# Forgetting attention with a gated FFN: the causal mask as rows of the score contraction

## The chip, the cores and the metric

The kernel runs on one core of a Trainium2 chip. A core has a matrix engine (TensorE, PE in the profile), a vector engine (VectorE, DVE), an activation engine (ScalarE, ACT), a general engine (GpSimd, POOL) and a queue engine (SyncE, SP), each of which works through its own instructions in order; here nearly all DMAs are issued by SP. The metric is the device time of one execution in microseconds; less is better. It is given as the median of the runs.

## What is computed

Eight batches of eight heads, 576 positions, head dimension 64. Attention with a decay that is a cumulative sum of log f, a causal mask, and then a feed-forward part over the heads side by side (512 channels, 1024 hidden), gated by the sigmoid of a three-tap convolution along the sequence:

```
scores = scale * q @ k.T
decay  = cum[:, :, :, None] - cum[:, :, None, :]      # cum = cumsum(log(clip(f, 1e-4, 1)))
scores = where(key later than query, -1e9, scores + decay)
x      = softmax(scores) @ v                          # heads side by side: 512 channels
h      = relu(x @ w_in)
out    = (h * sigmoid(conv3(h, conv_w))) @ w_out
```

## The kernel before

**Work.** Attention goes by half batches, hb 0 to 15, of four heads each; the FFN goes by batches b 0 to 7 once both half batches are done. Scores are made with keys on the partitions. The five diagonal blocks of a head (four of 128x128, one of 64x64) and the off-diagonal ones are separate groups: `sd` makes the diagonal blocks of two heads, `so` the off-diagonal ones of one head, `st` the 64x64 tails of four heads. `ed`, `eo` and `et` are their exponentials on ACT (L353, L370, L332). `pv` multiplies with v (L389, L394; a column of ones gives the softmax sum), `n` and `m` normalise on VectorE (L403, L405), `t` turns the result on PE (L414) and `tx` copies it (L417). Per batch and 128 hidden channels ff, `f` is the first FFN matmul (L429), `r` the relu (L440, ACT), `c` and `d` the two convolution steps (L446, L448, VectorE), `a` the tanh or sigmoid (L451, ACT), `g` the gate (L458, or L456 for the last ones, VectorE). `o` is the second matmul (L474), `e` copies it out (L479, L484), `s` stores it.

**How q and k come in.** A tile `qk` (a ring of four) holds q and k of a half batch with the contraction on 128 partitions. The fp32 input is read as pairs of 16-bit words and transposed by the DMA (L180): the odd partitions then hold the upper words, which are q or k in bf16, and the even ones hold the lower words, which are no use. Those 64 even rows are taken for other things. Three of them carry the decay: q rows hold cum or one, k rows the counterpart, so that the score matmul adds the decay by itself. The other even rows must be zero. In hb 2 to 7 VectorE multiplies by a mask of odd partitions and sets the ones (`cl`, L186), and `rw` writes the decay rows by DMA from an image in DRAM (L202, L203). In hb 8 to 15 a DMA writes zeros over 60 even rows (L194) and another the four rows of the image (L196); SP does it all in `fi`. Half batches 0 and 1 are loaded plainly, turned by PE (`tp`, L166) and copied out by ACT or VectorE with the same clamp (`cl`, L172, L174). hb 0 gets its decay by two more matmuls a score block (L315, L317).

**How the mask is made.** In hb 0 to 7 (`MASK_PE`) a matmul of an identity with a tile of 0 and -1e30 (L320) opens each group of diagonal blocks: one of 512 columns for four blocks, one of 256 for the tails. In hb 8 to 15 the exponentials of the diagonal blocks are written unmasked in fp32 (`pd`, `p3`), and POOL selects them into the fp16 tile with zeros above the diagonal (`md`, `mt`, L356, L335).

**What sets the order.** A long hand-written table, ORDER, lists all tasks; each engine gets its instructions in that order, and buffers are handed out by it. `PSUM` is four tiles of 1024 columns, taken by every group of scores, every `pv`, `t`, `f` and `o`. `x@DVE` in the table names the engine where there is a choice.

## Time and profile before

| | us |
|---|---|
| median of 3 runs | 247.38 |
| lowest, highest | 247.0, 248.49 |
| span of the profiled execution | 244.1 |
| between span and median | 3.3 |

The span runs from the first to the last instruction of the profiled execution, whose own time outside the profiler isn't listed; the rest up to the median is taken as a constant around the span. The profile gives for each group of instructions the line, the engine, the operation and what it writes and reads, the count, the busy time, the mean duration, and the idle time of the engine ahead of it with what ended that idle time. Consecutive instructions of an engine overlap in their records, so the duration of one in a dense stream is read from start to start.

### The profile page before, as it was taken

Reading aid. Unit: us, or ns where it says so; the run is one execution under the profiler, and the core shown is the slowest. Engines: PE = TensorE matmul, PEld = TensorE weight load, DVE = VectorE, ACT = ScalarE, POOL = GpSimd, SP = SyncE. Lnnn points to the kernel's source line nnn. Section 1 sums busy time; section 2 is a strip of 40 time slices with the busy share of each in tenths; the row PEclk is TensorE's granted clock in tenths of the full one; section 3 lists DMA queues with packets and bytes.
Section 4 is the critical chain, followed back from the end, with each engine's and each line's share of the span. In section 5 each row is a group of like instructions: output and inputs, shape, how many; then the busy total and the mean of one; then the engine's idle time right before and its main releaser. Section 6 shows DMA issues by size and latency. Waiting matters only on the chain.

```text
span 244.1 us, 6385 instructions
## 1 busy us (share of the span) xinstructions
PE 226.9 (93%) x2627; PEld 145.0 (59%) x2627; DVE 205.1 (84%) x323; ACT 206.9 (85%) x278; POOL 52.9 (22%) x77
## 2 busy tenths in 40 slices
PE   0899899779999999999999999999999999999991
PEld 0787585547556676575557755675666566444440
DVE  5735359999998999999999889996998889999931
ACT  2868677999998999999999999999988995798442
POOL 8020520205220020030402570245311311000000
PEclk9999999999999999999999999999999999999999
DMA  6999999999999999999999999969999950641326
GB/s 192 328 159 243 304 204 192 202 253 279 204 188 205 228 158 240 229 314 186 198 256 246 187 209 257 273 134 222 194 260 188 236 140 3 168 157 62 142 86 216
DMA packets 120176, 49.68 MB, mean 204 GB/s; under 512 B 109759, under 2 KB 110271, under 8 KB 120147
## 3 DMA queue, kind: packets, MB, share of 16 engines
q1 hardware_dynamic: 119981, 48.97, 92.4%
q8 instruction: 20, 0.33, 0.6%
q10 hardware_dynamic: 166, 0.31, 0.4%
q14 instruction: 9, 0.07, 0.1%
HBM read 21.11 MB, written 10.17 MB: 128 GB/s over the span
## 4 chain that ended last, share of the span: by engine, by line
PE 78%; DVE 7%; DMA 6%; ACT 4%; issue 1%; ACTq 1%; SPq 1%; DVEq 0%
PE ps L474 24%; PE ps L429 20%; PE ps L312 15%; PE ps L389 7%; DMA qk<-in_q_dram 3%; PE ps L320 3%; PE ps L394 3%; PE ps L166 2%; PE ps L414 2%; DVE u L446 2%; ACT pp L370 2%; DMA pd<-in_moe_conv_w_dram 2%; DVE u L448 2%; DVE qk L186 1%; DMA qk<-image 1%
## 5 line engine op out<-in xcount | busy, mean ns | idle before, releaser
L429 PE MATMUL ps<-xt,w_in_f 128*128 128x512 f16 (+1 forms) x512 | 69.9, 286 | 0.0
L370 ACT ACTIVATE pp<-ps 128x1024 f16<-128x1024 f32 x64 | 64.7, 1032 | 4.2 <-PE ps L312 2.7
L474 PE MATMUL ps<-w_out_f,hg 128*128 128x512 f16 x288 | 66.8, 379 | 0.0
L312 PE MATMUL ps<-qk 128*128 128x128 bf16 (+2 forms) x576 | 63.4, 240 | 1.6 <-ACT pp L353 0.8
L446 DVE SCALAR_TENSOR_TENSOR u<-ht,cwt 128x576 f32<-128x576 f16 x64 | 52.7, 837 | 3.6 <-ACT ht L440 3.4
L451 ACT ACTIVATE hg<-u,cw 128x576 f16<-128x576 f32 x64 | 48.7, 782 | 5.9 <-DVE u L448 5.8
L448 DVE SCALAR_TENSOR_TENSOR u<-ht,cwt,u 128x576 f32<-128x576 f16 x64 | 53.2, 846 | 0.5
L429 PEld LDWEIGHTS <-w_in_f 128*128 128x128 f16 x512 | 34.3, 98 | 28.5
L312 PEld LDWEIGHTS <-qk 128*128 128x128 bf16 x576 | 39.2, 98 | 19.8 <-issue 3.3
L440 ACT ACTIVATE ht<-ps 128x576 f16<-128x576 f32 x64 | 41.0, 663 | 6.0 <-DVE hg L458 2.7
L474 PEld LDWEIGHTS <-hg 128*128 128x128 f16 x288 | 26.9, 98 | 28.8
L458 DVE SCALAR_TENSOR_TENSOR hg<-hg,ht 128x576 f16<-128x576 f16 x51 | 38.7, 771 | 0.6 <-ACT hg L451 0.5
L356 POOL TENSOR_SCALAR_AFFINE_SELECT pp<-pd 128x1024 f16<-128x1024 f32 x16 | 19.7, 1244 | 53.6 <-ACT pd L353 53.6
L389 PE MATMUL ps<-va,pp 128*128 128x65 f16 x640 | 24.8, 193 | 1.1 <-DVE va L217 1.0
L389 PEld LDWEIGHTS <-pp 128*128 128x128 f16 x640 | 22.6, 97 | 3.7 <-DVE va L217 1.3
L405 DVE TENSOR_TENSOR xm<-ps,rc 128x896 f16<-128x896 f32 (+1 forms) x32 | 23.9, 751 | 0.5
L353 ACT ACTIVATE pp<-ps 128x1024 f16<-128x1024 f32 x16 | 16.6, 1039 | 4.7 <-PE ps L312 3.9
L353 ACT ACTIVATE pd<-ps 128x1024 f32<-128x1024 f32 x16 | 16.2, 1023 | 1.2 <-PE ps L312 1.0
L217 POOL CAST va<-vf 128x1024 f16<-128x1024 f32 x8 | 10.0, 1252 | 32.1 <-DMA vf<-in_v_dram 27.8
L320 PE MATMUL ps<-mask,ident 128*128 128x512 bf16 (+1 forms) x40 | 14.3, 359 | 1.5 <-ACT pp L370 0.8
L403 DVE RECIPROCAL rc<-ps 128x14 f32<-128x14 f32 (+1 forms) x32 | 6.7, 208 | 8.6 <-PE ps L394 5.5
L479 ACT COPY ob<-ps 128x1024 f32<-128x1024 f32 (+1 forms) x14 | 12.9, 919 | 0.3 <-issue 0.2
(83 smaller groups left out, 176.4 us busy)
## 6 DMA issues: line engine op xcount, KB each, us to landing
vf<-in_v_dram SPq DMA_DIRECT2D x32, 256.0 KB, 7.7
out_dram<-ob SPq DMA_DIRECT2D x14, 512.0 KB, 3.7
qk<-blank SPq DMA_DIRECT2D x8, 540.0 KB, 6.2
ob<-in_moe_w_in_dram SPq DMA_DIRECT2D x4, 512.0 KB, 6.3
ob<-in_moe_w_out_dram SPq DMA_DIRECT2D x4, 512.0 KB
out_dram<-ob SPq DMA_DIRECT2D x6, 256.0 KB, 7.2
vf<-in_v_dram SPq DMA_DIRECT2D x8, 128.0 KB, 5.9
hg<-in_q_dram SPq DMA_DIRECT2D x2, 288.0 KB
```

The costliest lines, as they stand in the source:

```text
L312: nc.tensor.matmul(o, tk[:, h * S + k0:h * S + k0 + 128], tq[:, h * S + q0:h * S + q0 + n], start=first, stop=last and not by_matmul(hb, h))
L353: nc.scalar.activation(o, ps_of(f"sd{i}").rearrange("p (s c) -> p s c", s=2), AF.Exp, scale=SCALE)
L370: nc.scalar.activation(pair(i)[:, s, 512:1536], ps_of(f"so{i}.{s}"), AF.Exp, scale=SCALE)
L389: nc.tensor.matmul(ps[:, c:c + D + 1], block(hb, h, m, n), va[:, h, m, 0:D + 1], start=(m == 0), stop=(m == n))
L405: nc.vector.tensor_tensor(xm[:, CUT * D * u:CUT * D * u + nj * k * D].rearrange("p (j x d) -> p j x d", x=k, d=D), got[:, :, :, 0:D], r.un ...
L429: nc.tensor.matmul(ps[:, t0:t1], w_in_f16[:, cc, 128 * ff:128 * (ff + 1)], xt[:, cc // 2, x:x + t1 - t0], start=(cc == 0), stop=(cc == NCC ...
L440: nc.scalar.activation(ht_of(b, ff)[:, 2:2 + S], ps_of(f"f{b}.{ff}")[:, 0:S], AF.Relu, scale=1.0 if (b, ff) in LATE else 0.5)
L446: nc.vector.scalar_tensor_tensor(u, ht[:, 1:1 + S], cwt[:, ff, 0:1], ht[:, 2:2 + S], op0=ALU.mult, op1=ALU.add)
L448: nc.vector.scalar_tensor_tensor(u, ht[:, 3:3 + S], cwt[:, ff, 1:2], u, op0=ALU.mult, op1=ALU.add)
L451: nc.scalar.activation(hg_of(b, ff), u_t[slot[f"c{b}.{ff}", "u"]], AF.Sigmoid if (b, ff) in LATE else AF.Tanh, scale=cw[:, ff, 1:2])
L458: nc.vector.scalar_tensor_tensor(hv, hv, 1.0, ht_of(b, ff)[:, 2:2 + S], op0=ALU.add, op1=ALU.mult)
L474: nc.tensor.matmul(ps[:, 512 * (c % 2):512 * (c % 2 + 1)], w, w_out_f16[:, ff, :], start=(ff == 0), stop=(ff == NFF - 1))
```

## The change

The mask becomes part of the score contraction in hb 1 to 15. Sixty rows beside q and k now hold steps of powers of two (`steps_q`, `steps_k`, made at the start by VectorE from counters that POOL lays out), such that the products sum to a large negative number where the key of a diagonal block is later than the query, and to next to nothing elsewhere. Only hb 0 keeps the mask matmul.

- hb 1: rows 64 to 123 of its `qk` tile hold the steps (`edge_rows` spreads them over the heads), 124 to 127 the decay rows.
- hb 2 to 7 (`BLEND`): VectorE clears the even rows (`blanked`, `cl`) and adds the tile `edge` in a second pass (`blend`, `cb`).
- hb 8 to 15: the DMA that wrote zeros writes the steps from a DRAM copy, `shape`.
- The decay rows are four in every half batch, with q and k sides in one DMA (`rows_of`).
- hb 0 and 1 are turned as bf16 alone, 64 rows, and copied without the clamp.
- The selects on POOL with their fp32 tiles go; the exponentials write fp16 directly. `st` and `et` use 64 partitions.
- f is loaded by SP (`lf`), behind one load of k, and the conv weights go first on ACT's queue. `sel_k` and `sel_q` are made by POOL, in place of VectorE.
- ORDER is another one; engines of copies and casts in it change too.

```diff
 ORDER = """
-dca cw ld0 ld1 ld0.0.0 tp0.0.0 dcl ld0.1.0 ld0.0.1 tp0.0.1 tp0.1.0 v0.0 ld0.1.1
+ld0 ks ld1 ld0.0.1 lf ld0.0.0 ld1.0.0 ld1.0.1 cw pz ld0.1.1 ld0.1.0 gu dca mk dcl gw
...
+    BLEND = (2, 3, 4, 5, 6, 7,)
-    MASK_PE = (0, 1, 2, 3, 4, 5, 6, 7,)
...
-            nc.tensor.transpose(o[:, 128 * j:128 * (j + 1)], i[:, 128 * j:128 * (j + 1)], ident_b)
+            nc.tensor.transpose(o[0:64, 128 * j:128 * (j + 1)], i[:, 128 * j + 1:128 * (j + 1):2], ident_b)
...
-    def clamp(hb, h0, nh, side):
-        t = (stq_t, stk_t)[side][hb % RING].bitcast(U16)[:, h0 * S:(h0 + nh) * S]
-        nc.vector.tensor_scalar(t, t, lim[:, 2 * side:2 * side + 1], lim[:, 2 * side + 1:2 * side + 2],
-                                op0=ALU.mult, op1=ALU.add)
+    def blanked(hb, side):
+        t = (stq_t, stk_t)[side][hb % RING].bitcast(U16)[:, 0:HS]
+        nc.vector.tensor_scalar(t, t, lit[:, 2:3], None, op0=ALU.mult)
+
+    def blend(hb, side):
+        t = (stq_t, stk_t)[side][hb % RING][:, 0:HS].rearrange("p (h s) -> p h s", h=HH)
+        nc.vector.tensor_tensor(t, t, edge[:, side].unsqueeze(1).broadcast_to((128, HH, S)), op=ALU.add)
+
+    def edge_rows(side, e):
+        copy = {"ACT": nc.scalar.copy, "POOL": nc.gpsimd.tensor_copy, "DVE": nc.vector.tensor_copy}[e]
+        o = qk_t[1][64:128, HS * side + S:HS * (side + 1)].rearrange("p (h s) -> p h s", s=S)
+        copy(o, qk_t[1][64:128, HS * side:HS * side + S].unsqueeze(1).broadcast_to((64, HH - 1, S)))
...
     def fill(hb):
-        nc.sync.dma_start(even_rows(hb, 4, 60, 0, 2 * HS).rearrange("p (h s) -> p h s", s=2 * S),
-                          blank.unsqueeze(1).broadcast_to((60, HH, 2 * S)))
+        nc.sync.dma_start(rows(qk_t[hb % RING], 0, 2, 60, 0, 2 * HS).rearrange("p (a h s) -> p a h s", a=2, s=2 * S),
+                          shape.rearrange("p a h s -> p a (h s)").unsqueeze(2).broadcast_to((60, 2, 2, 2 * S)))
+        rows_of(hb)
...
-    nc.scalar.dma_start(fsb[0:BH], f.rearrange("b h s -> (b h) s"))
-    nc.scalar.dma_start(fsb[BH:128], f.rearrange("b h s -> (b h) s"))
     nc.scalar.preload_act_table(AF.Ln)
     nc.scalar.dma_start(cwrow, moe_conv_w)
+    def load_f():
+        for h in range(2):
+            nc.sync.dma_start(fsb[BH * h:BH * (h + 1)], f.rearrange("b h s -> (b h) s"))
...
+    def steps_q():
+        nc.vector.tensor_scalar(near, count, GROUP + (FAR + 0.003) / STEP, None, op0=ALU.min)
+        nc.vector.scalar_tensor_tensor(bits, near, float(-128 * STEP), base, op0=ALU.mult, op1=ALU.add)
+        nc.vector.scalar_tensor_tensor(there, near, 0.0, bits, op0=ALU.is_ge, op1=ALU.mult)
+        nc.vector.scalar_tensor_tensor(dense[0], near, GROUP - 0.5, there, op0=ALU.is_le, op1=ALU.mult)
+
+    def steps_k():
+        nc.vector.tensor_scalar(bits, bits, -1.0, float(128 * (FIRST - STEP + 2 * 127) + 32768), op0=ALU.mult, op1=ALU.add)
+        nc.vector.scalar_tensor_tensor(dense[1], near, 1.0, bits, op0=ALU.is_ge, op1=ALU.mult)
+
+    def spread():
+        t = qk_t[1][64:128, 0:2 * HS].rearrange("p (a c) -> p a c", a=2)[:, :, 0:S]
+        nc.sync.dma_start(bass.AP(tensor=edge.tensor, offset=int(edge.offset), ap=[[2 * 2 * S, 64], [S, 2], [1, S]]), t)
...
+    def shapes():
+        even = bass.AP(tensor=edge.tensor, offset=int(edge.offset), ap=[[2 * 2 * S, 60], [S, 2], [1, S]])
+        for h in range(2):
+            nc.sync.dma_start(shape[:, :, h], even)
...
     def diag_scores(i):
...
-            if on:
+            if hb == 0:
                 masked(ps[:, 512 * s:512 * (s + 1)], 4, 128)
...
-    def diag_mask(i):
-        nc.gpsimd.affine_select(pair(i)[:, :, 0:512].rearrange("p s (m j) -> p s m j", j=128),
...
+                if hb in BLEND:
+                    add(f"cl{hb}.{side}", "DVE", [f"q{hb}.{side}"], lambda hb=hb, side=side: blanked(hb, side))
+                    add(f"cb{hb}.{side}", "DVE", [f"cl{hb}.{side}", "pe"], lambda hb=hb, side=side: blend(hb, side))
+            if hb in BLEND:
+                add(f"rw{hb}", "SP", ["ki", "zc"] + [f"cb{hb}.{side}" for side in range(2)], lambda hb=hb: rows_of(hb))
             else:
+                add(f"rw{hb}", "SP", ["ki", "zc", "zs"] + [f"q{hb}.{side}" for side in range(2)], lambda hb=hb: fill(hb))
```

Line numbers move by a few: the convolution steps are L446 and L448 before, L450 and L452 now, the gate is L458 and L462, the norm L405 and L409, the score matmul L312 and L332, the clamp or blanking L186 and L179; the add is L183.

On VectorE, at the first convolution steps of batch 0: `qk_85` is the q and k tile of hb 4, `u`, `ht` and `hg` are the FFN's tiles. Before:

```order
L186 TENSOR_SCALAR qk_88<-qk_88,lim 128x2304 x2
L446 SCALAR_TENSOR_TENSOR u_120<-ht_115,cwt 128x576
L448 SCALAR_TENSOR_TENSOR u_120<-ht_115,cwt,u_120 128x576
L186 TENSOR_SCALAR qk_85<-qk_85,lim 128x2304
L446 SCALAR_TENSOR_TENSOR u_121<-ht_117,cwt 128x576
L446 SCALAR_TENSOR_TENSOR u_122<-ht_116,cwt 128x576
L448 SCALAR_TENSOR_TENSOR u_121<-ht_117,cwt,u_121 128x576
L458 SCALAR_TENSOR_TENSOR hg<-hg,ht_115 128x576
```

The same place on VectorE now, from the first blanking of hb 4 on:

```order
L179 TENSOR_SCALAR qk_85<-qk_85,lit 128x2304
L183 TENSOR_TENSOR qk_85<-qk_85,edge 128x2304
L450 SCALAR_TENSOR_TENSOR u_117<-ht_112,cwt 128x576
L450 SCALAR_TENSOR_TENSOR u_118<-ht_113,cwt 128x576
L452 SCALAR_TENSOR_TENSOR u_117<-ht_112,cwt,u_117 128x576
L450 SCALAR_TENSOR_TENSOR u_119<-ht_114,cwt 128x576
L179 TENSOR_SCALAR qk_85<-qk_85,lit 128x2304
L452 SCALAR_TENSOR_TENSOR u_118<-ht_113,cwt,u_118 128x576
L183 TENSOR_TENSOR qk_85<-qk_85,edge 128x2304
```

Each pass over a side of a tile is now followed by a second one, the add, and both stand among the convolution steps.

On PE, where the tails of hb 1 (`qk_86`) follow an off-diagonal group, before:

```order
L312 LDWEIGHTS qk_86
L312 MATMUL ps_129<-qk_86 128x192
L320 LDWEIGHTS ident
L320 MATMUL ps_131<-mask,ident 128x256
L312 LDWEIGHTS qk_86
L312 MATMUL ps_131<-qk_86 128x64
```

The tails of hb 1 on PE now:

```order
L332 MATMUL ps_127<-qk_86 128x320
L332 LDWEIGHTS qk_86
L332 MATMUL ps_127<-qk_86 128x192
L332 LDWEIGHTS qk_86
L332 MATMUL ps_128<-qk_86 64x64
```

The mask's weights and its matmul of 256 columns are gone from between them.

On SP's queue, the first DMAs of the program; `hg` holds the plain loads of hb 0 and 1, `qk_87` is the tile of hb 2, `kc` the decay rows. Before:

```order
L159 DMA hg<-in_q_dram 128x576 x2
L159 DMA hg<-in_k_dram 128x576
L209 DMA vf_89<-in_v_dram 128x8x64
L159 DMA hg<-in_k_dram 128x576
L159 DMA hg<-in_k_dram 128x2x576
L159 DMA hg<-in_q_dram 128x2x576
L209 DMA vf_89<-in_v_dram 128x8x64 x3
L209 DMA vf_89<-in_v_dram 64x8x64
L180 DMA_TRANSPOSE qk_87<-in_k_dram 128x2304
L279 DMA image<-kc 64x576 x3
```

SP's first DMAs now:

```order
L157 DMA hg<-in_k_dram 128x576
L226 DMA u_117<-in_f_dram 64x576 x2
L157 DMA hg<-in_q_dram 128x576
L157 DMA hg<-in_q_dram 128x2x576
L157 DMA hg<-in_k_dram 128x2x576
L157 DMA hg<-in_k_dram 128x576
L157 DMA hg<-in_q_dram 128x576
L267 DMA edge<-qk_86 64x2x576
L303 DMA image<-signs 64x2x576
L304 DMA image<-signs 64x2x576
L173 DMA_TRANSPOSE qk_87<-in_k_dram 128x2304
```

f, the edge tile and two sign images stand ahead of the first transposing load, and the loads of v have moved behind it.

228 lines of the change are left out of this document (99 added, 129 removed).

## Prediction

> **What bounds the kernel now.** I read the page first, then the kernel cut at the first matmuls of the second stage for each batch, then PE's waits. The page's head says how full PE is, and its chain that PE carries most of it.
>
> ```profile
> span 244.1 us, 6385 instructions
> PE 226.9 (93%) x2627; PEld 145.0 (59%) x2627; DVE 205.1 (84%) x323; ACT 206.9 (85%) x278; POOL 52.9 (22%) x77
> PE 78%; DVE 7%; DMA 6%; ACT 4%; issue 1%; ACTq 1%; SPq 1%; DVEq 0%
> ```
>
> Next the busy time of PE, weight loads, DVE (VectorE), ACT (ScalarE) and POOL (GpSimd) in five stretches. The cuts: 38.7 is the first gated-FFN instruction on VectorE, 61 the first FFN matmul of batch 1, 193.3 that of batch 6, 234 the end of VectorE's last gate.
>
> ```profile
> 0.00:38.70 38.70, 30.35 (x415) 24.41 (x416) 20.35 (x48) 25.52 (x26) 11.88 (x38) 1.00 1.06 233
> 38.70:61.00 22.30, 18.97 (x272) 13.00 (x270) 21.99 (x34) 21.25 (x31) 5.29 (x4) 1.00 1.11 241
> 61.00:193.30 132.30, 132.29 (x1570) 84.16 (x1568) 123.49 (x181) 126.18 (x172) 32.26 (x32) 1.00 1.06 218
> 193.30:234.00 40.70, 40.60 (x358) 21.52 (x356) 37.65 (x61) 32.05 (x48) 3.50 (x5) 1.00 0.40 113
> PE ps L389 <- DVE va L217: 1.0, 1, 1.0
> PE ps L294 <- DMA pd<-in_moe_conv_w_dram: 7.2, 1, 7.2
> ```
>
> Three regimes, then. The start is a string of loads and waits. From 38.7 to 61 VectorE is full (21.99 of 22.30) and PE is not; the longest wait of PE after the first load is for a VectorE cast, and it falls there. From 61 on PE is full (132.29 of 132.30) and VectorE has some 7 us of idle per hundred. So a cut on PE is worth its whole length behind 61, and nothing in front of it, where an addition on VectorE costs its whole length.
>
> **What goes from PE.** The mask matmuls of half batches 1 to 7: 28 of 512 columns and 7 of 256; the five of half batch 0 stay. A matmul's recorded duration overlaps the next, so I take start to start.
>
> ```profile
> 57.37 0.39 PE L320 MATMUL ps<-mask,ident 128*128 128x512 bf16 x1
> 57.60 0.28 PE L312 MATMUL ps<-qk 128*128 128x128 bf16 x2
> 59.93 0.27 PE L320 MATMUL ps<-mask,ident 128*128 128x256 bf16 x1
> 60.04 0.28 PE L312 MATMUL ps<-qk 128*128 128x64 bf16 x4
> L320 PE MATMUL ps<-mask,ident 128*128 128x512 bf16 x12 | 4.6, 380 | 0.0
> L320 PE MATMUL ps<-mask,ident 128*128 128x256 bf16 x3 | 0.8, 272 | 0.0
> ```
>
> That is 0.23 and 0.11 us: 28 x 0.23 + 7 x 0.11 = 7.2 us over the kernel. The last two rows are those from 61 to the end: 12 x 0.23 + 3 x 0.11 = 3.1. What is saved ahead of 61 shows as other work pulled forward: in the orders, 47 off-diagonal score groups and 22 diagonal ones stand behind batch 1's first FFN matmul before, 41 and 20 now. The chain has both groups, four and eight matmuls long, and PE's last stretch:
>
> ```profile
> 62.18 0.44 PE ps L312 x4
> 105.55 0.45 PE ps L312 x8
> 61.04 0.62 PE L429 MATMUL ps<-xt,w_in_f 128*128 128x512 f16 x3
> 226.57 12.10 PE ps L474 x56
> ```
>
> 6 x 0.44 + 2 x 0.45 = 3.5. Behind its first batch 1 matmul PE now needs 238.67 - 61.04 = 177.63 us; it will need 3.1 + 3.5 = **6.6 less, 171.0**. The transposes and score matmuls keep their count and columns, so I cost the narrower outputs (64 rows) at nothing.
>
> **What comes on VectorE.** Per half batch 2 to 7 the two clamps (L186) become two blankings of the same shape, and two adds of 128x2304 bf16 follow. No row shows that add. Nearest is the last gate, an add-like two-tensor operation on 16-bit tiles; start to start it takes 0.37 for 576.
>
> ```profile
> 226.13 0.46 DVE L456 TENSOR_TENSOR hg<-hg,ht 128x576 f16<-128x576 f16 x1 [0.20 <-ACT hg L451]
> 226.50 0.81 DVE L448 SCALAR_TENSOR_TENSOR u<-ht,cwt,u 128x576 f32<-128x576 f16 x1
> 49.55 0.88 DVE L186 TENSOR_SCALAR qk<-qk,lim 128x2304 uint16<-128x2304 uint16 x1
> 50.35 0.81 DVE L446 SCALAR_TENSOR_TENSOR u<-ht,cwt 128x576 f32<-128x576 f16 x1
> 51.08 0.75 DVE L458 SCALAR_TENSOR_TENSOR hg<-hg,ht 128x576 f16<-128x576 f16 x1
> 51.74 1.08 DVE L405 TENSOR_TENSOR xm<-ps,rc 128x896 f16<-128x896 f32 x1
> L405 DVE TENSOR_TENSOR xm<-ps,rc 128x896 f16<-128x896 f32 x16 | 17.4, 1087 | 0.3
> L405 DVE TENSOR_TENSOR xm<-ps,rc 128x256 f16<-128x256 f32 x16 | 6.6, 415 | 0.2
> ```
>
> The two sizes of L405 differ by 640 elements and 672 ns, 1.05 ns an element. At that rate the gate's 576 would be 0.60 alone, so it runs faster; at twice the rate they are 0.30, and 0.07 is fixed. 2304 elements so take 2304 x 0.525 + 70 = 1.28 us. Bounds: the clamp's 0.80 (49.55 to 50.35) below, and above all of it at L405's large size, 1087 x 2304/896 = 2.80. I take 1.28, since the gate has the add's engine form and element size. Twelve make 15.4 us. The Trainium skill, "VectorE: DVE Perf Modes", section "The perf-mode tier table", speaks against such an add: a one-tensor operation on 16-bit data reaches four elements a cycle, a two-tensor one only two, 1224 ns for 2048. An estimate in proportion to that figure is 1.38 for 2304 and would make the forecast 0.3 us longer; no run here shows it yet.
>
> Between the first conv instruction and the last norm that batch 1's matmul needs, VectorE's order has 3 adds more, one L458 more, one L448 less, one cast less and one xt copy less (it goes to ACT, behind it).
>
> ```profile
> 38.86:60.69 21.83, 18.50 (x267) 12.73 (x266) 21.52 (x34) 20.95 (x31) 4.98 (x4) 1.00 1.11 241
> L217 DVE CAST va<-vf 128x1024 f16<-128x1024 f32 x1 | 0.7, 678 | 0.0
> 60.02 0.75 DVE L417 COPY xt<-ps 128x1152 f16<-128x1152 f16 x1
> 60.69 0.92 DVE L448 SCALAR_TENSOR_TENSOR u<-ht,cwt,u 128x576 f32<-128x576 f16 x1
> 56.79 1.12 ACT L417 COPY xt<-ps 128x1152 f16<-128x1152 f16 x1
> 86.88 0.50 PE ps L414 x9
> ```
>
> 3 x 1.28 + 0.66 - 0.73 - 0.68 - 0.67 = +2.4, so that norm ends at 60.69 + 2.4 = 63.1 where the copy ended before. Then the turn on PE (0.50), the copy on ACT (1.12) and the 0.35 from copy to matmul (60.69 to 61.04): **65.0, 4.0 later**. The other waiters there are PE's score groups queued in order behind the turn, and ACT behind them.
>
> Behind that norm VectorE has four adds, three 128x1024 output copies, one L448 and one small cast more, and one clamp, one L458, one xt copy and one 128x512 copy less.
>
> ```profile
> L479 DVE COPY ob<-ps 128x1024 f32<-128x1024 f32 x3 | 3.7, 1218 | 2.0 <-ACT xt L417 1.9
> L219 DVE CAST va<-vf 64x256 f16<-64x256 f32 x4 | 1.0, 261 | 0.0
> L484 DVE COPY ob<-ps 128x512 f32<-128x512 f32 x2 | 1.4, 691 | 3.4 <-PE ps L474 2.1 <-ACT ob L484 1.3
> ```
>
> 4 x 1.28 + 3 x 1.22 + 0.73 + 0.26 - 0.80 - 0.66 - 0.67 - 0.69 = +6.9 (L446 to L458 start to start, 0.73 for L448). Now VectorE is busy for 123.49 + 37.65 = 161.1 of the 173 us from 61 to 234, idle for 11.9; it will need 168.0, less what it gets back from POOL (2.5, below). PE's 171.0 end 4.7 after VectorE's last gate (234 to 238.67), so from 63.1 there are 168.2 us for those 165.5: 2.7 of idle, if PE never waits. I take it that VectorE keeps about 4, and PE so waits **1.5 us**; the ends are nothing (no wait of PE is listed behind 61) and 6.
>
> **What goes from POOL and ACT.** The 24 selects of half batches 8 to 15 vanish; the exponentials write the same tile sizes, so ACT gains nothing. POOL was idle most of the time, so its own gain is nothing. Its reads cost VectorE something:
>
> ```profile
> 119.14 2.99 POOL L356 TENSOR_SCALAR_AFFINE_SELECT pp<-pd 128x1024 f16<-128x1024 f32 x2 [7.39 <-ACT pd L353]
> 119.52 1.65 DVE L448 SCALAR_TENSOR_TENSOR u<-ht,cwt,u 128x576 f32<-128x576 f16 x1
> ```
>
> This L448 took 1.65 instead of 0.81: 0.84 lost to a pair of large selects. Eight such pairs would be 6.7, the upper bound of what VectorE gets back; nothing is the lower, where the selects meet operations that they don't hold up. I take 2.5, three such meetings; it is in the idle above.
>
> **The start.** f comes by SP behind one k load, and no longer by ACT ahead of the conv weights; the edge image (SP waits for VectorE's six step operations and POOL's memsets) and two sign images now stand ahead of the first transposing load; all eight turned tiles are copied ahead of the scores. The rows that gate it:
>
> ```profile
> 2.05 4.98 DMA pd<-in_moe_conv_w_dram
> 22.71 3.01 DMA qk<-image
> ```
>
> The conv weights can go 1.25 us earlier (2.05 against 0.80), and the row image no longer waits for a weight load on SP; against that, four turned tiles of nine transposes (0.50 each, as the turn's) come ahead of the first exponential, and SP stands still for the edge. I take the first conv to stay at 38.9; both ends are 2 us.
>
> **Sum.** 65.0 + 171.0 + 1.5 = 237.5 for PE's last matmul, and 244.1 - 238.67 = 5.4 behind it as now: a span of 242.9, 1.2 less. The median before is 247.38, 3.3 above the span; so **246.2 us**. With the start's 2 us and 0 to 3 of waits this case alone spans 243.5 to 249.
>
> **Rivals.**
>
> First, the start shortens by its 2 us and VectorE gets all collisions back, so that PE's 1.5 of waits falls too: 246.2 - 3.5 = 242.7. For it speaks the earlier issue of f and of the conv weights; against it that the scores then wait for four more turned tiles. The Trainium skill, "SBUF — State Buffer", section "Who interferes with whom", has an exclusive lock between VectorE operations with two SBUF inputs and POOL operations that read SBUF, the loser blocked to the end. The 0.84 above agrees with it in direction. By that rule the adds themselves can be held by POOL's casts, which stay, so it helps this rival only where selects were what VectorE met.
>
> Second, the other side: VectorE becomes the bound to the end. Its 11.9 us of idle are waits for results of ACT and PE and do not shrink by themselves. If nine of them stay, the span is 63.1 + 165.5 + 9 + 10.1 (behind 234) = 247.7, or 251.0. It costs PE time from 2.7 of idle up, and the kernel is slower than before from 5.4 up. For it speaks that 21.52 of 21.83 us are busy already in the early stretch; against it the same figure: where VectorE sets the pace, its idle nearly goes.
>
> Third, the add runs at its upper bound of 2.80: 1.52 more for each of the seven behind 38.9, 10.6 us on an engine that has no room: 257.
>
> Fourth, nothing gained: the DMA share of 1.06 to 1.11 says that the loads are back to back up to 193, and PE's gain could turn into waits for q and k: 247.4.
>
> **Chances.** Forecast case 0.50; first rival 0.22; second 0.17; third 0.06; fourth 0.05. One per cent, 2.5 us, is about what a measurement here can tell from no change; the forecast case lies on both sides of 244.9, with 0.14 below it, 0.35 within and 0.01 above. Faster: 0.14 + 0.22 = 0.36. Within 1%: 0.35 + 0.04 of the second + 0.05 = 0.44. Slower: 0.01 + 0.13 + 0.06 = 0.20. The range begins at 241.2, the first rival with 1.5 of the 4.0 hidden as well, and ends at the second's 251.0; a lower part of the first, half of the second and the third are left out, two in ten.
>
> **What would show it.** The add near 1.28 start to start; the first FFN matmul of batch 1 near 65 with VectorE full ahead of it; PE's work from there near 171 with 1 to 2 us of waits; VectorE's idle behind 63 near 4. Wrong would be a batch 1 matmul at 61 or earlier, a first conv away from 38.9 by more than 2, or waits of PE on VectorE of several us.

## The result, and the profile after

The changed kernel takes 261.55 us in the median of 4 runs (260.38 to 262.48), the kernel before 247.31 on the same chip: a ratio of 1.0555, 95% interval 1.0506 to 1.0605. It is slower by 14 us where 246.2 was forecast. The profiled execution of the changed kernel took 260.38 and has a span of 258.6, 14.5 over that of before. Medians of the runs below leave out any execution over 1.5% slower than the fastest of its kernel.

The head of the page after, its first rows of busy time, and the first row of its chain of waits:

```profile
span 258.6 us, 6297 instructions
PE 226.8 (88%) x2592; PEld 144.5 (56%) x2592; DVE 231.0 (89%) x332; ACT 204.8 (79%) x275; POOL 48.4 (19%) x64
PE 58%; DVE 24%; ACT 5%; DMA 4%; issue 4%; SPq 2%; POOL 1%; ACTq 0%; DVEq 0%; POOLq 0%
```

VectorE is 25.9 us busier; its share of the chain of waits rose by 17 points, and PE's fell by 20. Where the time went is read best from windows cut at the same events: the first FFN matmuls of batches 0, 1 and 2, and the end of VectorE's last gate. Columns: the stretch and its length, busy time (count) of PE, weight loads, VectorE, ScalarE, GpSimd, the granted PE clock, the DMA share, GB/s. First before, cut so:

```profile
0.00:36.77 36.77, 28.42 (x401) 23.37 (x402) 18.42 (x46) 24.59 (x25) 11.88 (x38) 1.00 1.08 237
36.77:61.04 24.27, 20.94 (x288) 14.08 (x287) 23.96 (x36) 22.23 (x33) 5.29 (x4) 1.00 1.08 233
61.04:89.56 28.52, 28.51 (x331) 18.12 (x329) 26.76 (x40) 26.98 (x37) 4.52 (x4) 1.00 1.07 204
89.56:234.20 144.64, 144.54 (x1595) 87.60 (x1595) 134.54 (x202) 131.42 (x183) 31.24 (x31) 1.00 0.87 191
234.20:244.10 9.90, 4.46 (x21) 1.84 (x19) 1.40 (x3) 1.71 (x4) 0.00 (x0) 0.98 0.56 186
```

The same five stretches of the kernel after:

```profile
0.00:40.48 40.48, 28.77 (x395) 24.75 (x396) 33.09 (x49) 25.56 (x29) 17.63 (x41) 1.00 0.92 218
40.48:72.53 32.05, 22.92 (x313) 15.58 (x312) 29.84 (x40) 28.03 (x37) 9.40 (x7) 1.00 1.12 203
72.53:102.13 29.60, 26.63 (x330) 16.96 (x330) 29.57 (x37) 24.63 (x35) 12.89 (x10) 1.00 0.95 211
102.13:248.60 146.47, 143.87 (x1540) 85.38 (x1538) 137.84 (x209) 124.43 (x173) 8.49 (x7) 1.00 0.89 186
248.60:258.60 10.00, 4.62 (x21) 1.83 (x19) 0.69 (x1) 2.15 (x4) 0.00 (x0) 0.88 0.36 135
```

The lengths differ by 3.7 (start), 7.8 (batch 0's stretch), 1.1 (batch 1's), 1.8 and 0.1: 14.5 in all, 12.6 of it ahead of batch 2. Those first two batches are a regime of their own. There VectorE has 59.4 of 61.7 us busy now, and had 50.7 of 52.8 before; from batch 2 on it had, and has, room.

Where the adds stand in the kernel after, by the view of one tile's instructions (durations min/median/max in ns, first and last start in us):

```profile
L183 DVE TENSOR_TENSOR qk<-qk,edge x12: 1290/1350/1360, 22.7 to 94.4; 128x2304 bf16<-128x2304 bf16 x12
```

And its timeline of VectorE at one of them, which also shows the first convolution step (start, length):

```profile
42.96 1.36 DVE L183 TENSOR_TENSOR qk<-qk,edge 128x2304 bf16<-128x2304 bf16 x1
44.23 2.32 DVE L450 SCALAR_TENSOR_TENSOR u<-ht,cwt 128x576 f32<-128x576 f16 x2
```

From 42.96 to 44.23 the add takes 1.27 us start to start; the forecast had 1.28. But all twelve stand between 22.7 and 94.4, that is ahead of batch 2, and the first convolution step comes at 44.23, not 38.9.

PE's matmuls behind batch 1's first, in the kernel before; columns: count | busy, mean ns | idle before, with its releasers:

```profile
L312 PE MATMUL ps<-qk 128*128 128x128 bf16 (+4 forms) x411 | 41.8, 241 | 0.0
L320 PE MATMUL ps<-mask,ident 128*128 128x512 bf16 (+1 forms) x15 | 5.4, 358 | 0.0
```

In the kernel after, by the same view:

```profile
L332 PE MATMUL ps<-qk 128*128 128x128 bf16 (+3 forms) x368 | 37.6, 241 | 4.1 <-DVE u L450 1.7 <-DMA qk<-image 0.7 <-ACT ht L444 0.7
L433 PE MATMUL ps<-xt,w_in_f 128*128 128x512 f16 x448 | 60.5, 286 | 0.8 <-ACT xt L421 0.4 <-DVE xm L409 0.4
```

The work did go: 15 masks and some 40 score matmuls. With each matmul counted at the median start-to-start time of its kind, an estimate, PE's work from batch 1's first matmul on fell from 174.4 to 168.5 us. Its waits rose from 2.9 to 12.5, about half of them too short to show as idle, since the recorded ends of matmuls overlap the next starts.

### The profile page after: what moved, and what is told of

Its sections match the earlier page's. It is cut to its first block, busy times and chain, and to the rows that moved or that the text cites. A ratio compares the mean times of both kernels' runs of the same rounds, so it can differ in the third digit from the quotient of the medians.

```text
span 258.6 us, 6297 instructions
## 1 busy us (share of the span) xinstructions
PE 226.8 (88%) x2592; PEld 144.5 (56%) x2592; DVE 231.0 (89%) x332; ACT 204.8 (79%) x275; POOL 48.4 (19%) x64
## 4 chain that ended last, share of the span: by engine, by line
PE 58%; DVE 24%; ACT 5%; DMA 4%; issue 4%; SPq 2%; POOL 1%; ACTq 0%; DVEq 0%; POOLq 0%
PE ps L478 20%; PE ps L433 16%; PE ps L332 11%; PE ps L393 5%; DVE u L450 5%; DVE u L452 4%; DVE hg L462 3%; DVE qk L183 2%; ACT pp L374 2%; DVE xm L409 2%; DMA vf<-in_v_dram 2%; DMA hg<-in_q_dram 2%; PE ps L398 2%; DVE qk L179 2%; PE ps L418 2%
## 5 line engine op out<-in xcount | busy, mean ns | idle before, releaser
L332 PE MATMUL ps<-qk 128*128 128x128 bf16 (+3 forms) x576 | 61.8, 241 | 10.1 <-DMA qk<-image 3.8
L374 ACT ACTIVATE pp<-ps 128x1024 f16<-128x1024 f32 x64 | 64.5, 1029 | 5.0 <-PE ps L332 4.3
L452 DVE SCALAR_TENSOR_TENSOR u<-ht,cwt,u 128x576 f32<-128x576 f16 x64 | 55.1, 875 | 0.4
L450 DVE SCALAR_TENSOR_TENSOR u<-ht,cwt 128x576 f32<-128x576 f16 x64 | 53.7, 856 | 0.4 <-ACT ht L444 0.4
L332 PEld LDWEIGHTS <-qk 128*128 128x128 bf16 (+1 forms) x576 | 37.7, 99 | 28.3 <-issue 10.8
L364 ACT ACTIVATE pp<-ps 128x1024 f16<-128x1024 f32 x32 | 32.3, 1028 | 8.6 <-PE ps L332 4.9
L462 DVE SCALAR_TENSOR_TENSOR hg<-hg,ht 128x576 f16<-128x576 f16 x51 | 38.8, 781 | 0.4 <-ACT hg L455 0.3
L216 POOL CAST va<-vf 128x1024 f16<-128x1024 f32 x10 | 14.9, 1506 | 118.2 <-DMA vf<-in_v_dram 111.7
L393 PEld LDWEIGHTS <-pp 128*128 128x128 f16 x640 | 22.7, 97 | 5.3 <-issue 2.6
L409 DVE TENSOR_TENSOR xm<-ps,rc 128x896 f16<-128x896 f32 (+1 forms) x32 | 23.7, 750 | 0.4
L183 DVE TENSOR_TENSOR qk<-qk,edge 128x2304 bf16<-128x2304 bf16 x12 | 16.1, 1346 | 0.1
L164 PE MATMUL ps<-ident_b,hg 128*64 128x128 bf16 x72 | 7.9, 309 | 6.0 <-DMA hg<-in_q_dram 4.6
L179 DVE TENSOR_SCALAR qk<-qk,lit 128x2304 uint16<-128x2304 uint16 x12 | 10.5, 872 | 2.1 <-DMA qk<-in_q_dram 2.0
L483 ACT COPY ob<-ps 128x1024 f32<-128x1024 f32 (+1 forms) x11 | 9.9, 899 | 2.2 <-PE ps L478 1.4
L164 PEld LDWEIGHTS <-hg 128*64 128x64 bf16 x72 | 7.6, 175 | 6.3 <-DMA hg<-in_q_dram 4.7
```

The lines of the kernel that those rows point to most:

```text
L332: nc.tensor.matmul(o, tk[:, h * S + k0:h * S + k0 + m], tq[:, h * S + q0:h * S + q0 + n], start=first, stop=last and not by_matmul(hb, h))
L364: nc.scalar.activation(pair(i)[:, :, 0:512], ps_of(f"sd{i}").rearrange("p (s c) -> p s c", s=2), AF.Exp, scale=SCALE)
L374: nc.scalar.activation(pair(i)[:, s, 512:1536], ps_of(f"so{i}.{s}"), AF.Exp, scale=SCALE)
L393: nc.tensor.matmul(ps[:, c:c + D + 1], block(hb, h, m, n), va[:, h, m, 0:D + 1], start=(m == 0), stop=(m == n))
L409: nc.vector.tensor_tensor(xm[:, CUT * D * u:CUT * D * u + nj * k * D].rearrange("p (j x d) -> p j x d", x=k, d=D), got[:, :, :, 0:D], r.un ...
L450: nc.vector.scalar_tensor_tensor(u, ht[:, 1:1 + S], cwt[:, ff, 0:1], ht[:, 2:2 + S], op0=ALU.mult, op1=ALU.add)
```

## The experiments

Three theories at first: V, VectorE's own time sets the pace; L, the loads in SyncE's queue do; O, the searched order and the start cost the time by themselves. All ratios are against the kernel before on the same chip.

**masks_back: the adds out, masks on PE again.** It leaves the mask rows of half batches 2 to 7 at zero and masks them by matmul.

```diff
-                    add(f"cb{hb}.{side}", "DVE", [f"cl{hb}.{side}", "pe"], ...blend(hb, side))
...
-        if hb == 0:
+        if hb == 0 or hb in BLEND:
             masked(ps_of(f"st{hb}")[0:SL, 0:HH * SL], HH, SL)
...
```

> The changed kernel with its twelve adds taken out and the causal mask of half batches 2 to 7 put back as mask matmuls (24 of 512 columns and 6 of 256); order and start otherwise as they are. Theory V, VectorE sets the time from the first conv on: seven of the twelve adds stand behind the first conv, 7 x 1.27 = 8.9 us of VectorE's work, and the matmuls (about 3 us behind batch 1's first FFN matmul) fill stalls that PE has anyway (9.6 us more than before), so the time falls from 261.5 to 251 to 253. Rival O, the start and the searched order cost the time and the adds are hidden: 259.5 to 263.5. PE as the bound would make it slower by 3.

Measured: 258.43, ratio 1.041 (1.035 to 1.048): 3.1 us less than the changed kernel, against 9 expected by theory V and 2 at most by its rival O. Between the two batches' first matmuls, by windows:

```profile
41.84:73.56 31.72, 27.24 (x327) 17.69 (x326) 24.04 (x36) 28.05 (x37) 6.23 (x7) 0.95 1.19 207
73.56:102.21 28.65, 27.64 (x341) 17.52 (x341) 24.20 (x33) 24.74 (x35) 9.69 (x10) 1.00 1.07 230
```

VectorE is now idle for 7.7 us of the first stretch, and it is as long as with the adds (31.7 against 32.0). So the adds are not alone in holding it: 9.8 us of the loss against the kernel before (248.65 on that chip) are there without them.

**before_adds and free_adds: the same time on VectorE in the kernel before.** The first puts an add of zeros behind each clamp, the second puts adds that nothing waits for behind the second clamp of each half batch.

```diff
         nc.vector.tensor_scalar(t, t, lim[:, 2 * side:2 * side + 1], ...)
...
+        nc.vector.tensor_tensor(x, x, zero[:, 0:S].unsqueeze(1).broadcast_to((128, HH, S)), op=ALU.add)
...
+        for x in range(4 if clamped.count(hb) == 2 else 0):
+            nc.vector.tensor_tensor(zero[64:128], zero[64:128], zero[64:128], op=ALU.add)
```

> The kernel before, in its own order, with an add of a zero tile (128x2304, bf16) on VectorE behind each of the twelve clamps; the result does not change. Theory V: VectorE's idle of 19 us behind the first conv are short waits for ScalarE and PE, which an in-order queue cannot fill with adds, so most of the adds' 15.2 us shows: the time goes from 247.3 to 256 to 262. Forecast's model: three adds in the early stretch, 3.8 us, show whole, those behind take up idle: 250 to 252. Rival O, the adds are hidden: below 249.

> The kernel before with adds on VectorE that nothing waits for: four adds of a 64x1152 zero tile behind the second clamp of each half batch 2 to 7 (estimate 0.67 each by the forecast's rate, 16 us in all, as much as the twelve adds of the run before_adds), so that the row loads wait for the clamps alone and not for an add. Theory L, in before_adds the adds cost 14 us because SyncE's in-order queue stood still ahead of the row loads (19 us in the first 110) and every load behind came later: without that the time is 249 to 253. Theory V, VectorE's own time is what counts: 258 to 263, as before_adds' 261.8.

Measured: 261.77 (1.055, 1.047 to 1.064) and 266.42 (1.075, 1.071 to 1.079). In before_adds the twelve adds, 15.2 us, cost 13.1. The free adds took 19.6 us, not 16, each in place behind the last; their group's row in that run:

```profile
L192 DVE TENSOR_TENSOR zero<-zero 64x1152 bf16<-64x1152 bf16 x24 | 19.6, 815 | 0.8
```

And the stretches of batch 0, of batch 1 and from batch 2 on, by windows of the same run:

```profile
37.80:71.50 33.70, 24.79 (x288) 16.26 (x287) 31.54 (x44) 22.90 (x33) 5.46 (x5) 0.85 0.90 185
71.50:110.20 38.70, 30.52 (x331) 19.22 (x328) 36.49 (x52) 27.05 (x37) 3.70 (x3) 0.91 0.91 175
110.20:255.60 145.40, 144.65 (x1595) 87.49 (x1595) 134.59 (x202) 131.76 (x183) 31.20 (x31) 1.00 0.81 179
```

The time rose by 18.5 us for 19.6 of work. The two spans differ by more, 21.4, since that of the kernel before lies 3.9 us below the median on this chip and that of free_adds 0.9: 1.0 are in the start, 9.4 in batch 0's stretch, 10.2 in batch 1's, 0.8 behind. In that place VectorE's time is paid nearly whole, and it is not the row loads' wait for an add that costs: theory L for these two runs falls. Theory V's range was met by before_adds and exceeded by free_adds.

**late_adds: the same work behind batch 2.** Two such adds at gates of each of batches 2 to 6.

```diff
+        if 2 <= b <= 6 and ff % 4 == 1:
+            nc.vector.tensor_tensor(zero[64:128], zero[64:128], zero[64:128], op=ALU.add)
```

> The kernel before with ten adds of the 64x1152 zero tile on VectorE (0.75 to 0.82 us each as in free_adds, some 8 us in all), two behind gates of each of batches 2 to 6, so all behind batch 2's first FFN matmul. The result does not change. VectorE has 12.6 us of idle between there and batch 7's first matmul. Forecast's model, VectorE's idle covers them: 247.5 to 249.5. Theory V, VectorE's waits cannot be filled and each add is paid: 254 to 256.

Measured: 252.54, ratio 1.018 (1.014 to 1.023), 4.1 us more in the medians (3.4 to 5.7 by the interval) for 8.4 of work. The group of those adds:

```profile
L460 DVE TENSOR_TENSOR zero<-zero 64x1152 bf16<-64x1152 bf16 x10 | 8.4, 835 | 0.2
```

And the stretch from batch 2 to the last gate, by windows:

```profile
91.20:241.30 150.10, 146.79 (x1597) 88.03 (x1596) 143.63 (x212) 131.81 (x183) 31.76 (x31) 1.00 0.84 187
```

In that stretch, 144.64 long before, VectorE's idle fell from 10.1 to 6.5 and the length grew by 5.5. A third to a half is covered: neither the forecast's model nor its opposite holds.

**extra_loads: the loads alone.** Two copies of 0.59 MB each from DRAM to DRAM in SyncE's queue of the kernel before.

```diff
+        for x in range(2 if (hb, side) == (3, 0) else 0):
+            nc.sync.dma_start(spare[x], v[0, HH * x:HH * x + HH]...)
```

> The kernel before with two transfers more on SyncE's queue, 0.59 MB each, a copy of v's first half to spare DRAM that nothing reads, behind half batch 3's first transposing load (near 32 us). VectorE, PE and ScalarE have nothing more to do. Theory T, the loads are full up to batch 2's first matmul: 1.18 MB at 240 GB/s are 5 us, or up to twice that since they are also written to DRAM, so 251 to 257. Rival, the loads run ahead of need: within 1.5 us of 247.5.

Measured: 251.3, ratio 1.017 (1.011 to 1.024), 2.9 us more in the medians (2.6 to 5.9 by the interval) for 1.18 MB. In the profile batch 0's stretch is 4.4 longer (28.7 against 24.27), and VectorE is now idle for 4.9 of it; the start is 1.1 longer, but late_adds, which is the kernel before up to batch 2, has a start 1.3 longer, so that need not be an effect of the loads:

```profile
37.90:66.60 28.70, 23.71 (x288) 15.93 (x286) 23.77 (x35) 22.69 (x33) 3.41 (x4) 0.88 1.13 220
```

So the loads have little slack there either.

**fill_all and old_fill: no blanking, no adds, all mask rows by DMA.** The first in the new order, the second in that of the kernel before with a start like its own; old_order is the latter with the adds left in.

```diff
-    BLEND = (2, 3, 4, 5, 6, 7,)
+    BLEND = ()
```

> The changed kernel with half batches 2 to 7 treated as 8 to 15 are: no blanking and no add on VectorE, the 60 mask rows filled by DMA from the image of steps (six fills more of 0.55 MB; the image is written ahead of the first row load). Order otherwise as it is. VectorE has 24 us less to do, 15 of it behind the first conv. Theory V: 246 to 250. Theory L, the loads set the time up to batch 2: four of the six fills (2.2 MB, some 10 us at 215 GB/s) come ahead of batch 2's loads, and the time is 256 to 264. Theory O, the new order alone holds the first two batches back: 257 to 261, as masks_back's 258.4.

> As old_order, with no blanking and no adds: half batches 2 to 15 all get their mask rows by DMA. Against the kernel before VectorE loses twelve clamps (9.6 us) and PE the mask matmuls (7 us), and the DMA engines move 3.3 MB more. Theory V: 238 to 244. Theory L, loads set the pace early: the first batches come up to 10 us later, and the time is 248 to 258.

> The changed kernel's work, adds included, in the order of the kernel before: each add right behind its blanking, fills where they stood, and a start like that of before (half batch 0 turned first, v loaded early, the edge image loaded behind the first two transposing loads). Theory O, the searched order and its start cost the 14 us: 247 to 252. Theories V and L, the adds cost what they cost in that order too (before_adds 261.8) less up to 7 us of mask matmuls on PE: 255 to 262.

Measured: 271.76 (1.093, 1.086 to 1.101), 270.89 (1.093, 1.087 to 1.100) and 265.76 (1.071, 1.067 to 1.075). With 24 us less on VectorE fill_all is some 10 slower than the changed kernel: six more fills, 3.3 MB, and the wait for the image that they copy cost more than the adds. fill_all and old_fill are also above theory L's ranges, 256 to 264 and 248 to 258. How the fills and the wait divide was not separated; in old_fill the start alone is 11.9 longer than before:

```profile
0.00:48.70 48.70, 31.39 (x391) 25.46 (x392) 24.84 (x40) 23.56 (x25) 22.24 (x47) 0.93 0.90 213
```

The old order with the adds is some 4 slower than the new one, so theory O's number for it, 247 to 252, fails (that of V and L, 255 to 262, too), and the new order is the better one for this work. That does not clear the order and the start. The adds cost 13 us in the old order (before_adds) and 3 in the new one, and the new order, with its start and the rest of the change, costs 10 without any add (masks_back). The costs don't add up to 23: together they are 14.

**casts_on_act and five_casts: GpSimd's casts to ScalarE**, all those of v and of the weights in the first, five in the second (in ORDER `@POOL` becomes `@ACT`).

> The changed kernel with all casts of v and of the weights that GpSimd does moved to ScalarE, in the same places of the order. Theory V: VectorE loses about 10 us behind the first conv where its instructions overlap GpSimd's casts (1.5 us instead of 0.73 each); with no casts on GpSimd that goes and the time falls to 252 to 255, if ScalarE's queue takes some 17 us more work without holding the exponentials. Rival: ScalarE, whose casts now wait in order for v's loads, becomes late, and the time stays within 2 us of 261.5 or rises.

> The changed kernel with five of GpSimd's casts moved to ScalarE: those of w_out (three) and of v for half batches 4 and 5 that stand back to back between 72 and 88 us, where seven of VectorE's instructions took 1.5 us in place of 0.73. Theory V for that stretch (VectorE idles 0.1 us of 29.6 there): 4 to 5 us of collisions go and the stretch of batch 1 falls to 25.5 to 27, the time to 257.5 to 259. Rival: ScalarE's 4.7 us more of work hold the exponentials, or the loads hold batch 2: within 1.5 of 261.5.

Measured: 270.03 (1.090, 1.080 to 1.099) and 261.38 (1.053, 1.045 to 1.062). What the five casts met, by VectorE's timeline in the changed kernel:

```profile
83.27 3.09 DVE L450 SCALAR_TENSOR_TENSOR u<-ht,cwt 128x576 f32<-128x576 f16 x2
86.29 3.18 DVE L452 SCALAR_TENSOR_TENSOR u<-ht,cwt,u 128x576 f32<-128x576 f16 x3
```

And by GpSimd's there, with a lone cast as it shows ahead of them (in brackets the idle time before and its releaser):

```profile
79.54 1.04 POOL L522 CAST w_out_f<-ob 128x1024 f16<-128x1024 f32 x1 [4.51 <-DMA ob<-in_moe_w_out_dram]
81.50 5.76 POOL L522 CAST w_out_f<-ob 128x1024 f16<-128x1024 f32 x3 [0.93 <-DMA ob<-in_moe_w_out_dram]
```

Three casts without a pause last 5.76 where one alone takes 1.04, and two L450 beside them take 3.02 (83.27 to 86.29) in place of 1.46. Moving them gave VectorE its time back and cost ScalarE as much; batch 1's stretch in five_casts, by windows:

```profile
72.20:102.20 30.00, 26.53 (x331) 16.79 (x331) 27.11 (x38) 28.89 (x40) 5.35 (x5) 1.00 0.92 197
```

And in casts_on_act:

```profile
77.30:112.10 34.80, 28.38 (x330) 17.45 (x330) 26.21 (x39) 31.41 (x45) 0.00 (x0) 0.95 0.86 193
```

In five_casts VectorE's 29.57 became 27.11, ScalarE's 24.63 became 28.89 of 30.00, and the stretch did not get shorter. With the five casts ScalarE is nearly full in VectorE's place; without them it had 5 us of idle, so that it was short of time before is not shown. The rival's numbers came out in both runs.

**loads_first and masks_loads: SyncE's order.** In ORDER:

```diff
-... pe ... zc q2.1 v0.0 q2.0 ... wi3 ... q5.1 ... v1.0 v1.1 rw4 ... q5.0 ... v1.3 v1.2 ... v1.4
+... q2.1 v0.0 q2.0 pe zc ... wi3 v1.0 v1.1 v1.3 v1.2 v1.4 q5.1 ... rw4 ... q5.0
```

> The changed kernel with only SyncE's order altered: the edge image and the two sign images, for which SyncE stood still 4.8 us at 5.2, come behind the first two transposing loads and v's first, and all five loads of v for batch 1 come ahead of half batch 5's q and k. Theory B (two bounds at once between the first FFN matmul of batch 0 and that of batch 1: VectorE, 27.4 us of work and 1.5 of collisions in 32.0, and the loads): VectorE alone then still needs 29 to 30 us there, so batch 1 comes 2 to 4 us earlier, half of it from the start, and the time is 257.5 to 260. Theory L, loads alone: 5 to 8 earlier, 254 to 257. Theory V, VectorE alone: no change, 260.5 to 262.5.

> masks_back (no adds, the masks of half batches 2 to 7 on PE) with the same new order of SyncE as loads_first. Theory B: with the adds gone VectorE has 11 us of idle between the two batches' first matmuls, so that only the loads hold it; with the loads earlier that stretch falls from 31.7 to 25 to 27 us and the time from 258.4 to 250 to 253. Theory L, loads alone: as much gained as loads_first gains. Theory V: within 1.5 us of 258.4.

Measured: 261.39 (1.053, 1.045 to 1.061) and 258.66 (1.043, 1.033 to 1.052): nothing gained with or without the adds, against the numbers of theory B and, in loads_first, of theory L. Theory V's number, no change, came out in both, but not by its mechanism: in masks_loads VectorE is idle for 7.1 us of batch 0's 33.1. What had gone from v's wait came back as a wait for rows; PE's waits for loads in batch 0's stretch, here of the changed kernel (us in total, times, longest):

```profile
PE ps L332 <- DMA qk<-image: 3.0, 2, 2.1
PE ps L393 <- POOL va L216: 2.1, 1, 2.1
PE ps L433 <- POOL w_in_f L522: 1.7, 1, 1.7
```

And of loads_first:

```profile
PE ps L332 <- DMA qk<-image: 5.0, 1, 5.0
```

**exps_later, masks_exps, adds_all, masks_all: the exponentials.** In batch 0's stretch ScalarE has six exponentials more than before (18 against 12 by the groups of ScalarE there), because half batch 4's and 5's scores were pulled forward. These runs move half batch 5's behind batch 1's first matmuls, alone and together with the other changes.

```diff
-... sd10 ... ed10 ... sd11 ed11 ... so10.0 ... so11.1 ... eo10.0 ... so11.0 ... eo11.0 f1.0 f1.1 eo11.1
+... f1.0 f1.1 sd10 ed10 sd11 ed11 so10.0 eo10.0 so11.1 so11.0 eo11.0 eo11.1
```

> The changed kernel with half batch 5's two diagonal score groups, three of its off-diagonal ones and their five exponentials moved behind batch 1's first FFN matmuls on PE and ScalarE; nothing else. Theory T (VectorE, ScalarE and the loads are each nearly full from batch 0's first FFN matmul to batch 1's): VectorE still needs some 29.5 us, so the stretch falls from 32.0 only to 30 to 31 and the time to 260 to 261.5. Theory E, ScalarE's exponentials alone hold it: 27 to 28 us and a time of 256.5 to 258.5.

> masks_loads (no adds, masks of half batches 2 to 7 on PE, SyncE's loads of v early) with the same exponentials moved. Theory T: now none of the three is full, and the stretch falls from 33.1 to 27 to 29 us, the time from 259.3 to 253 to 256. If it stays above 31, something else holds it, PE's in-order wait for half batch 4's rows among the candidates, and the time stays within 2 us of 259.

> The changed kernel, adds left in, with start_kc's start, loads_first's loads and exps_later's exponentials together. Theory T: the start gives 0.5 to 2, the rest little while VectorE has its adds: 258 to 260.5. Theory E or L: 252 to 256.

> As adds_all without the adds, the masks of half batches 2 to 7 on PE. Theory T: 251 to 254, so that against adds_all the adds cost 5 to 8 us where nothing else is full, more than the 3.1 that they cost in the order as it was. If the adds' price stays at 3, VectorE is not what holds the early stretch even then.

Measured: 263.72 (1.069, 1.058 to 1.080), 265.01 (1.069, 1.061 to 1.077), 266.07 (1.072, 1.064 to 1.081) and 265.48 (1.071, 1.065 to 1.077). In exps_later, batch 0's and batch 1's stretches by windows:

```profile
40.49:69.20 28.71, 21.71 (x285) 14.25 (x283) 28.59 (x37) 24.24 (x33) 7.50 (x6) 0.94 1.00 199
69.20:104.44 35.24, 31.32 (x361) 19.28 (x360) 30.91 (x39) 28.47 (x39) 13.30 (x10) 0.95 0.92 188
```

Batch 0's stretch falls by 3.3 and stops where VectorE is full (28.59 of 28.71); the next one grows by 5.6. The work has to be done ahead of batch 2 in any case. Without the adds (masks_exps, masks_all) the stretch stays at 32 to 33, in masks_all with one wait of PE of 4.5 us for half batch 4's rows, which the earlier loads of v had pushed back. In masks_exps no engine is full there:

```profile
41.01:72.66 31.65, 23.64 (x295) 15.23 (x294) 24.04 (x34) 24.54 (x33) 9.18 (x8) 0.94 1.08 210
```

With the DMA share at 1.08, the loads and the in-order waits for them are the nearest candidate; no run settles it. Theory T's numbers for these runs were wrong. The pair adds_all and masks_all differs by 0.6 only, within its noise: with the loads in that order the adds cost nothing that these runs can tell.

**start_old and start_kc: the start.** start_old turns half batch 0's tiles first and begins its scores; start_kc makes the decay rows ahead of the k steps and moves GpSimd's large memset away from them. The copy of step rows that was to go from VectorE to ScalarE in start_old stayed on VectorE. The second's edit of ORDER:

```diff
-... cw pz ... gu dca mk dcl gw tp1.0.0 tp0.0.0 dcs tp0.0.1 cl0.0.1@DVE pe ... dck ... pm ... ed1 ... ed0
+... cw pz ... gu dca mk dcl tp1.0.0 tp0.0.0 tp0.0.1 dcs dck cl0.0.1@DVE gw ... (pm ahead of ks) ... ed0 ed1
```

> The changed kernel with its start put in another order: the four tiles of half batch 0 are turned first and its scores begin, half batch 1's loads and turns come between its score groups, one of the two copies of step rows goes from VectorE to ScalarE's idle place by its earlier neighbours. Theory S, the four turned tiles of half batch 1 that stand ahead of the first scores (36 transposes, 3.8 us, and a wait of 1.4) are what moved the first conv from 38.9 to 44.2: the first exponential comes at 14 to 17 instead of 22.3, the first conv at 39 to 41, and, as VectorE is full from there, the time falls by 3 to 5, to 257 to 258. Rival: VectorE's preparation (34 us busy of the first 43) or the loads set the first conv: the exponential comes earlier, the first conv stays at 43 to 45, and the time within 1.5 us.

> The changed kernel with another order of the start alone: VectorE makes the decay rows ahead of the step rows for k, GpSimd's large memset comes before its other work and no longer beside the decay rows, the first exponential of half batch 0 goes ahead of the second, and the edge and sign images come behind the first transposing loads on SyncE. Theory S, VectorE's preparation (with 3.5 us lost beside GpSimd's memsets) sets the start: the decay rows end near 11.6 instead of 15.8, the first exponential comes at 17 to 20 instead of 22.3, the first FFN matmul at 37 to 39 instead of 40.5, and the time falls by 2 to 3.5. Rival, the turned tiles and the loads set it: the first FFN matmul stays at 40 to 41 and the time within 1 us.

Measured: 263.68 (1.062, 1.055 to 1.068) and 261.07 (1.052, 1.044 to 1.059). The decay rows' first instruction, by VectorE's timeline in the changed kernel:

```profile
12.59 2.38 DVE L294 TENSOR_SCALAR kc<-u 128x576 bf16<-128x576 f32 x1
```

Beside it, by GpSimd's timeline there:

```profile
12.63 2.01 POOL L548 MEMSET qk<- 64x2304 f32 x1
```

In start_kc, VectorE's timeline at the same instruction:

```profile
8.99 1.12 DVE L294 TENSOR_SCALAR kc<-u 128x576 bf16<-128x576 f32 x1
```

And ScalarE's at the first exponential:

```profile
17.81 1.02 ACT L364 ACTIVATE pp<-ps 128x1024 f16<-128x1024 f32 x1 [0.77 <-PE ps L336]
```

The rows end 4.9 us earlier (10.91 against 15.76), the first exponential at 17.8 instead of 22.3, and the first FFN matmul at 40.0 instead of 40.5. In start_old the exponential is at 18.9, that matmul at 43.7 and the first conv at 47.0, later than both forecasts had it. So neither the preparation nor the four turned tiles alone set the first FFN matmul.

## Why the prediction was wrong, step by step

The span was forecast at 242.9 and is 258.6, 15.7 more. Cut at the same events, 3.7 of that are the start, 3.8 batch 0's stretch (4.0 longer forecast, 7.8 found) and 8.2 all that follows batch 1's first matmul (177.9 forecast, 186.1 found). Of the 3.3 us that the sum adds to the span, 1.7 to 1.8 lie around it in every run whose time and span are both listed; the rest is how far the profiled execution of the kernel before lay below the median.

**PE's work** was right: 6.6 us less forecast behind batch 1's first matmul, 5.9 found. None of it became time.

**The add** was right, 1.27 against 1.28 (12 x 1.27 = 15.2). The Trainium skill, "VectorE: DVE Perf Modes", section "The perf-mode tier table", has 1224 ns for a two-tensor bf16 operation of 2048 elements; the estimate of 1.38 for 2304 that follows from it was a little high here. The rate that gave 1.28 is no general one: it gave 0.67 for the free adds, which took 0.82 on average as recorded.

**The early stretch** was nearly right for what it counted: from the first convolution step to the last norm that batch 1 needs, 24.2 us were forecast and 25.7 found (44.23 to 69.93). Collisions with GpSimd's casts, 3.2 us in batch 0's stretch against 0.7 before, are enough for the difference.

**"The first conv stays at 38.9, both ends 2 us"** failed by 5.4, of which 3.7 had already arisen by batch 0's first FFN matmul. VectorE is busy for 33.1 us of the start instead of 18.4: four adds are there, four blankings where two clamps stood, the step operations, and two instructions that waited out GpSimd's memsets. A fifth add stands just ahead of the first conv. The forecast counted the start's new instructions on SyncE and PE, did not add up VectorE's and put these five adds at nothing. That VectorE's work is what moved the start is not shown: start_kc took 1.9 us of it away and gained 0.5.

**"VectorE keeps about 4 of its idle, and PE so waits 1.5"** is the step that failed most. The 8.2 us behind batch 1's first matmul are this idle and, in about equal part, VectorE's work, which is 170.0 us from that last norm on instead of 165.5. From batch 1's first matmul to the last gate, by windows, first before, then after, then masks_back:

```profile
61.04:234.20 173.16, 173.05 (x1926) 105.72 (x1924) 161.30 (x241) 158.39 (x219) 35.76 (x35) 1.00 0.91 193
72.53:248.60 176.07, 170.50 (x1868) 102.34 (x1868) 167.41 (x245) 149.06 (x207) 21.38 (x17) 1.00 0.90 190
73.56:247.10 173.54, 171.23 (x1879) 102.92 (x1879) 160.42 (x239) 148.78 (x207) 17.51 (x17) 1.00 0.91 191
```

VectorE kept 8.7 of its 11.9 us of idle, not 4, and PE waited 12.5 us in all where 2.9 + 1.5 were counted. The 11.9 were taken over the whole 173 us, but every add stands ahead of 94.4. In those two batches VectorE had 0.3 and 1.8 us of idle before. free_adds shows that time added there is paid at 0.94 of its length, late_adds that even behind batch 2 half or more is. It does not follow that VectorE alone holds the changed kernel: masks_back takes 7.0 us of its work out of this stretch, puts the mask matmuls back on PE, and shortens it by 2.5.

**"The collisions give back 2.5"** had the wrong sign. VectorE's loss beside GpSimd, each instruction against the median of its kind, went from 6.1 to some 10 us behind the first convolution step, and from 1.7 to 7.5 in the stretches of the first two batches: the selects went, but 16 casts now fall into those stretches where 8 did, some without a pause between them.

**"Other work pulled forward"** was counted on PE alone, 0.44 for a score group. Each such group has an exponential on ScalarE of 0.9, and its q, k and rows must be loaded by then. Both had little room there: ScalarE was busy for 22.2 of 24.3, and the DMA share was 1.08. Ahead of batch 1 that is 5.4 us of ScalarE's time for the six exponentials, and v's last load for batch 1 is issued near 55 instead of 42, as SyncE's timeline shows, first before:

```profile
41.13 1.02 SPq L209 DMA_DIRECT2D vf<-in_v_dram  x2
```

And after:

```profile
53.94 2.67 SPq L208 DMA_DIRECT2D vf<-in_v_dram  x3
```

By the GB/s of the windows, 15.3 MB had been moved by batch 1's first matmul, against 14.4 before. At extra_loads' price, 2.6 to 5.9 us for 1.18 MB, an estimate of 2 to 5 us.

**The rivals.** The second, VectorE as the bound, came nearest: its condition, that nine of the 11.9 us of idle stay, held with 8.7, and in batch 1's stretch VectorE is full (29.57 of 29.60 us). Its sum was too small by the start and the work: 69.93 for the norm instead of 63.1, 170.0 of VectorE's work behind it instead of 165.5, 8.7 of idle and 10.0 behind the last gate give 258.6, where it had 247.7. The fourth, the loads, was priced as no gain; they cost time. Neither counted on both at once. The first had the start shorter, and it is longer; the third falls with the add's 1.27.

What is shown: an add takes as long as forecast, 12.6 of the 14.5 us are lost ahead of batch 2, and there, in the kernel before, neither VectorE nor the loads can take more work for free. In the changed kernel the adds taken out gave 3.1, and no run with loads, casts, exponentials or the start moved is clearly faster than it. That ScalarE holds the time is argued only, since no run adds work to it alone. What stays open: most of the 10 us that the changed kernel loses even without the adds, that is, what sets the first FFN matmul at 40 to 44 in the runs with the new start, and how the 7.8 us of batch 0's stretch divide between the loads, ScalarE and VectorE. No run with the new order made that stretch shorter than 28.7. No variant that was run beats the kernel before.

## What to carry to other kernels

Idle time covers added work only where that work stands: cut the profile at the events of the pipeline and compare the added work with the idle of its own stretch, not of the run. Work that is pulled forward brings its loads, its exponentials and the copies of its results with it, and each has to fit the engine and the queue at the new place. Where removing one load at a time shows little, add a known amount to each engine instead: where it is paid in full, the engine has no room.
